# Regrouping the q products around a burst of k^T v in a linear-attention block

## The chip, the cores and the metric

The kernel runs on one core of a Trainium2 chip. The core has several engines, each with its own list of instructions that it works through in order: TensorE (PE in the profile, with PEld for its weight loads) for matrix products into PSUM, VectorE (DVE), ScalarE (ACT) and GpSimd (POOL) for the elementwise work, and SyncE (SP), whose queue here issues the transfers. Engines wait for each other through semaphores. The metric is the device time of one execution in microseconds (us), without a profile; a profiled execution is a run of its own.

## The reference

The inputs are a sequence x of 2048 tokens with 640 features, and weights, all bf16. With 32 heads of 20 features each:

```
q, k, v = split(layernorm(x) @ wqkv)                 # 640 features each
phi(a)  = concat(softmax(a @ w_phi), softmax(-(a @ w_phi)))   # per head, 40 features
o       = phi(q) @ (phi(k)^T v) / (phi(q) @ sum(phi(k)) + 1e-6)
h       = x + o @ wo
out     = h + (gelu(layernorm(h) @ w_gate) * (layernorm(h) @ w_up)) @ w_down    # 1536 wide
```

The sum over all tokens in phi(k)^T v means that no token's o can be computed before every token's k and v have been.

## The kernel before, in words

The 2048 tokens lie in 16 tiles of 128 (t), four of which make a token block of 512 (b = 0 to 3). The 640 features lie in five chunks of 128 (c).

The first stage goes over the 16 tiles. It normalises them, writes them transposed (features on partitions) into `LN1T`, multiplies v and k, takes both exps of k on ACT into `E`, and divides by the sums in `k_norm` (the multiplication at L355 is on POOL, and for some tiles half of it on DVE). The product phi(k)^T v is accumulated over all tiles in one PSUM tile, `kvp`: `kv_tile(t)` (L374) makes 32 small products for one token tile. They are not made at once for each tile but in bursts: tiles 0 to 3 at t = 9, tiles 4 to 8 at t = 13 (`KVG`), tiles 9 to 12 at t = 15 (`KVQ`, the third burst), and tiles 13 to 15 after the loop.

q needs no sum over tokens. Its product with w_phi folded in is made as 20 units: unit 5b + c is chunk c of token block b, and takes five products of 128x512 (L396), one for each chunk of the contraction. `QG` lists the units in groups. A group of one or two units shares a PSUM tile; `q_mm(j)` multiplies group j (`part` picks units of it, `kcs` contraction chunks), and `q_exp(j)` takes exp and exp of the negative on ACT (L401) into the group's tile `Eq[j]`. `QT` says that groups 0 to 3 are made at t = 15 inside the loop. `KVQ = {1: (9, 10, 11, 12)}` puts the third burst right behind group 1.

After the loop a copy on POOL (L536) reads a column of `Eq[2]`'s negative exp and writes to the gate weights' tile, so that the first loads of `Wg` (L538, on SP's queue) are held back until then. Then come the burst of tiles 13 to 15 and `kv_mask` (L381, L383, on DVE), which turns `kvp` into the block form `KV` that the second stage multiplies with.

The second stage starts with the attention of single token tiles: `attn_a(t)` multiplies phi(q) of tile t with `KV` (L585, chunks 0 to 4 with the positive exp, then chunks 0 to 4 with the negative) and copies the sums to SBUF, `attn_b` to `attn_b3` divide on DVE and form o (L686), which is transposed into `oT`, `attn_c` multiplies by `Wo` (L707), and the rest prepares the second layernorm. The remaining groups of q fill PE between the first two tiles. Then follows the gated feed-forward part (`gate_up` L767, `down` L789), which holds most of the time, with the other tiles' attention woven in.

The order on PE and on SP's queue is the order of the calls in the source; nothing reorders it. PSUM tiles of two banks come from a pool of four (`gtile`), of which `kvp` holds one until `kv_mask` has read it. A new tile waits until the engine that reads the old one is through.

The edited place, before: at t = 15 in the loop groups 0 (units 5, 6), 1 (0, 1), the third burst, 2 (2, 3), 3 (4); after the loop the last burst, and group 4 (7, 8) with `attn_a(0, 1)` between its ninth and its tenth product. `Wo` is loaded at L534 from SP's queue at t = 13.

Of the kernel before, what the change touches and what calls it, by code (L numbers as in the profile page):

```python
# [11 lines left out]
ACTF = mybir.ActivationFunctionType  # L12
# [5 lines left out]
def kernel(  # L18
# [12 lines left out]
    nc = tc.nc  # L31
# [17 lines left out]
    LQ = (7, 8, 9, 9, 10)  # L49
    FQ = (10, 11, 12, 13, 14)  # L50

    QG = ((5, 6), (0, 1), (2, 3), (4,), (7, 8), (9, 10), (11, 12), (13, 14), (15,), (16,), (17,), (18,), (19,))
    QT = (15, 15, 15, 15)
    T3 = 3

# [39 lines left out]

    Eq = [const.tile([P, len(g), 2, 512], BF16, name=f"Eq{j}") for j, g in enumerate(QG)]
    ident = const.tile([P, P], BF16, name="ident")
# [5 lines left out]
    def eq(t, c, s):  # L103
        for E, g in zip(Eq, QG):
            if t // 4 * NC + c in g:
                return E[:, g.index(t // 4 * NC + c), s, t % 4 * P:(t % 4 + 1) * P]
# [4 lines left out]
    def gtile(name):  # L111
        return psG.tile([P, 2, 512], F32, name=name, tag="G")
# [272 lines left out]
    pqs = {}  # L385

    def q_mm(j, part=(0, 1), kcs=range(NC)):

        if 0 in part and 0 in kcs:
            pqs[j] = gtile("pq")  # L390
        for i, bc in enumerate(QG[j]):
            if i not in part:
                continue
            b, c = divmod(bc, NC)
            for kc in kcs:
                nc.tensor.matmul(pqs[j][:, i, :], lhsT=Wq2[:, kc, c * P:(c + 1) * P], rhs=LN1T[b][:, kc, :],  # L396
                                 start=(kc == 0), stop=(kc == NC - 1))

    def q_exp(j, signs=(0, 1)):
        for s in signs:  # L400
            nc.scalar.activation(Eq[j][:, :, s, :], pqs[j][:, 0:len(QG[j])], ACTF.Exp, scale=(1.0, -1.0)[s])  # L401

    def st_act(t, i):

# [89 lines left out]
    for t in range(NT):  # L494
# [13 lines left out]
        for j in range(len(QT)):  # L508
            if t == QT[j]:
                q_mm(j)  # L510
                q_exp(j)
                for i in KVQ.get(j, ()):
                    kv_tile(i)
# [21 lines left out]
    q = len(QT)  # L535
# [112 lines left out]
    def attn_a(t, dve=0):  # L648
        attn_a_mm(t)
        AB, ab = ABs[t % 2], st[t, "ab"]  # L650
        for u in ((1, 0) if t in (4,) else (0, 1)):
            (nc.vector.tensor_copy if u >= 2 - dve else nc.scalar.copy)(
                AB[:, :, u * UH:(u + 1) * UH].rearrange("p s (r h) f -> p r s (h f)", r=2),
                ab[u][:, :, 0:2 * QH * KC].rearrange("p r (s x) -> p r s x", s=2))
        st[t] = AB
# [173 lines left out]


    q_mm(q, (0,))
    q_mm(q, (1,), (0, 1, 2, 3))
    attn_a(0, 1)
    q_mm(q, (1,), (4,))
    q_exp(q)
    q_mm(q + 1)
    attn_b(0, True)
    attn_b2(0, True)
    attn_b3(0)
    load_up()  # L840
    attn_a(1, 0)
    q_exp(q + 1, (0,))
    q_mm(q + 2)
    q_exp(q + 1, (1,))
# [92 lines left out]
```

## Time and profile before

| | us |
|---|---|
| median of 3 runs (lowest, highest) | 271.64 (271.57, 271.98) |
| the profiled execution | 272.4 |
| its span, first to last instruction | 270.7 |
| PE busy | 265.7 (98%) |
| DVE, ACT, POOL busy | 174.9, 138.9, 101.2 |

In a row of the chain of waits stand the start, the length, and what the end of the program was waiting for then, with a count of merged instructions. In a row of a timeline stand start, length, engine, line, operation, the tiles written and read, their sizes, the count, and in brackets the idle time before it and what ended it. A row of waits has the total, the number and the longest. A row of a group by line has the count, the busy time, the mean of one in ns, and the idle time before. A row of a stretch has, for PE, PEld, DVE, ACT and POOL, the busy time and the number of instructions, then the granted clock, the DMA share and GB/s. A row of a DMA queue has packets, MB and the share of the 16 DMA engines' time.

### The profile page before, as it was taken

To read this page: it belongs to the slowest core of one execution; us is meant where nothing else is said; L and a number is where in the kernel's file an instruction comes from. 1 tells how busy PE (TensorE), PEld (TensorE's weight loads), DVE (VectorE), ACT (ScalarE), POOL (GpSimd) and SP (SyncE) were. 2 spreads that over 40 slices of the span, in tenths; PEclk is the share of its full clock that TensorE was granted. 3 is DMA by queue.
4 is the path that set the end of the run, shared out by engine and by line. 5 is a ranking of instruction groups with operands and counts; after the bars stand their busy time and mean duration, and the time that the engine had idled before them with its cause. 6 is when DMAs were issued, how large, how long until landed. Compare 5 with 4: busy or idle time off the path is not lost.

```text
span 270.7 us, 7046 instructions
## 1 busy us (share of the span) xinstructions
PE 265.7 (98%) x2867; PEld 171.3 (63%) x2867; DVE 174.9 (65%) x347; ACT 138.9 (51%) x249; POOL 101.2 (37%) x238
## 2 busy tenths in 40 slices
PE   7999999999999999999999999999999999999995
PEld 6777777755455877788755455775555476444574
DVE  5889999996877767876466783568673332333322
ACT  5789998876789675245541356421544300322100
POOL 5548988796002335376211564014661100000000
PEclk9999999999999999999999999999999999999999
DMA  6998257250678432442201222102222101000011
GB/s 187 225 199 169 54 99 110 38 150 2 234 246 244 155 101 56 41 104 51 52 24 51 48 50 51 48 3 75 77 44 52 24 24 51 24 0 0 4 48 48
DMA packets 45264, 22.10 MB, mean 82 GB/s; under 512 B 37808, under 2 KB 43184, under 8 KB 45232
## 3 DMA queue, kind: packets, MB, share of 16 engines
q1 hardware_dynamic: 44576, 21.64, 32.6%
q8 instruction: 22, 0.36, 0.6%
q10 hardware_dynamic: 656, 0.03, 0.2%
q14 instruction: 10, 0.08, 0.1%
HBM read 10.18 MB, written 2.62 MB: 47 GB/s over the span
## 4 chain that ended last, share of the span: by engine, by line
PE 96%; DMA 2%; SPq 0%; issue 0%; DVE 0%
PE gu L767 39%; PE pd L789 19%; PE pq L396 8%; PE pk L296 8%; PE po L707 8%; PE pv L296 7%; PE kvp L374 2%; PE pv L312 2%; DMA Wv<-in_A_wqkv_dram 2%; PE ab L618 1%; PE wa L248 1%; PE ab L585 1%; PE tp L164 0%; SPq L193 0%; SPq L190 0%
## 5 line engine op out<-in xcount | busy, mean ns | idle before, releaser
L770 ACT ACTIVATE g<-gu 128x512 bf16<-128x512 f32 (+1 forms) x60 | 30.4, 510 | 73.8 <-PE gu L767 72.9
L773 DVE TENSOR_TENSOR GT<-gu,g 128x512 bf16<-128x512 f32 (+1 forms) x60 | 34.4, 580 | 46.7 <-PE gu L767 38.8
L767 PE MATMUL gu<-LN2T,Wg 128*128 128x512 bf16 (+1 forms) x300 | 61.8, 337 | 0.0
L767 PE MATMUL gu<-LN2T,Wu 128*128 128x512 bf16 (+1 forms) x300 | 61.7, 336 | 0.0
L789 PE MATMUL pd<-Wd,GT 128*128 128x320 bf16 (+4 forms) x396 | 53.9, 295 | 0.0
L789 PEld LDWEIGHTS <-GT 128*128 128x128 bf16 x396 | 37.6, 98 | 14.5 <-DVE GT L773 0.2
L767 PEld LDWEIGHTS <-Wu 128*128 128x128 bf16 x300 | 29.4, 98 | 22.6
L767 PEld LDWEIGHTS <-Wg 128*128 128x128 bf16 x300 | 29.0, 98 | 21.2
L296 PEld LDWEIGHTS <-LN1T 128*128 128x128 bf16 x290 | 27.9, 98 | 10.5
L355 POOL TENSOR_TENSOR E<-E,rs 128x640 bf16<-128x640 bf16 x25 | 31.6, 1299 | 4.4 <-DVE rs L351 4.1
L791 DVE TENSOR_TENSOR y<-pd,x_sb 128x320 bf16<-128x320 f32 (+4 forms) x33 | 15.8, 480 | 24.2 <-PE pd L789 24.2
L707 PE MATMUL po<-Wo,oT 128*128 128x320 bf16 x160 | 24.5, 299 | 0.0
L296 PE MATMUL pk<-Wk,LN1T 128*128 128x320 bf16 x160 | 24.4, 299 | 0.0
L396 PE MATMUL pq<-LN1T,Wq 128*128 128x512 bf16 x100 | 22.9, 379 | 0.0
L347 DVE TENSOR_REDUCE sk<-E 128x64 f32<-128x1280 bf16 x16 | 22.9, 1430 | 0.0
L401 ACT ACTIVATE Eq<-pq 128x1024 bf16<-128x1024 f32 (+1 forms) x26 | 19.9, 831 | 3.5 <-PE pq L396 3.3
L340 ACT ACTIVATE E<-pk 128x640 bf16<-128x640 f32 x28 | 18.7, 746 | 3.0 <-PE pk L296 3.0
L707 PEld LDWEIGHTS <-oT 128*128 128x128 bf16 x160 | 15.6, 98 | 7.3 <-ACT oT L165 0.2
L296 PE MATMUL pv<-Wv,LN1T 128*128 128x320 bf16 x130 | 19.8, 299 | 0.0
L151 ACT ACTIVATE ln<-x_sb,v,rstd 128x640 bf16<-128x640 bf16 x14 | 12.9, 920 | 13.4 <-POOL v L746 13.2
L396 PEld LDWEIGHTS <-Wq 128*128 128x128 bf16 x100 | 9.4, 98 | 10.3
L682 DVE TENSOR_TENSOR tt<-AB,w 128x1280 bf16<-128x1280 f32 x10 | 15.1, 1506 | 0.4 <-POOL w L675 0.3
(120 smaller groups left out, 290.6 us busy)
## 6 DMA issues: line engine op xcount, KB each, us to landing
out_dram<-y SPq DMA_DIRECT2D x15, 160.0 KB, 1.8
x_sb<-in_A_x_dram SPq DMA_DIRECT2D x6, 320.0 KB, 4.0
Wu<-in_B_w_up_dram SPq DMA_DIRECT2D x1, 1920.0 KB, 8.9
Wg<-in_B_w_gate_dram SPq DMA_DIRECT2D x2, 768.0 KB, 5.8
Wd<-in_B_w_down_dram SPq DMA_DIRECT2D x1, 1440.0 KB
Wo<-in_A_wo_dram SPq DMA_DIRECT2D x1, 800.0 KB, 5.2
x_sb<-in_A_x_dram SPq DMA_DIRECT2D x4, 160.0 KB, 3.3
Wv<-in_A_wqkv_dram SPq DMA_DIRECT2D x2, 320.0 KB, 4.2
```

The lines of the kernel that those rows point to most:

```text
L296: nc.tensor.matmul(ps[:, u, 0:HD], lhsT=lnT(t, c), rhs=W[:, c, u * HD:(u + 1) * HD], start=(c == 0), stop=(c == NC - 1))
L340: nc.scalar.activation(Ek[t][:, s, :].rearrange("p (u f) -> p u f", u=2), pk[:, :, 0:HD], ACTF.Exp, scale=((lnp[t][2], nrstd[t]) if t in C ...
L347: nc.vector.reduce_sum(sk, Ek[t].rearrange("p s (h f) -> p (s h) f", f=Dh), axis=AX.X)
L355: eng.tensor_tensor(e, e, rs[:, s * H:(s + 1) * H, None].to_broadcast([P, H, Dh]), ALU.mult)
L396: nc.tensor.matmul(pqs[j][:, i, :], lhsT=Wq2[:, kc, c * P:(c + 1) * P], rhs=LN1T[b][:, kc, :], start=(kc == 0), stop=(kc == NC - 1))
L401: nc.scalar.activation(Eq[j][:, :, s, :], pqs[j][:, 0:len(QG[j])], ACTF.Exp, scale=(1.0, -1.0)[s])
L707: nc.tensor.matmul(pos[u], lhsT=st[t][:, c, :], rhs=Wo[:, c, u * HD:(u + 1) * HD], start=(c == 0), stop=(c == NC - 1))
L767: nc.tensor.matmul(gu[i][:, 0:n], lhsT=W[:, c, f * P:(f + 1) * P], rhs=LN2T[b][:, c, a0:a1], start=(c == 0), stop=(c == NC - 1))
L770: nc.scalar.activation(g[:, 0:n], gu[0][:, 0:n], ACTF.Gelu_apprx_tanh)
L773: nc.vector.tensor_tensor(st[b, "g", f][:, a0:a1], gu[1][:, 0:n], g[:, 0:n], ALU.mult)
L789: nc.tensor.matmul(pd[:, 0:f1 - f0], lhsT=st[b, "g", f][:, tl * P:(tl + 1) * P], rhs=Wd[:, f, f0:f1], start=(f == 0), stop=(f == NF - 1), ...
L791: nc.vector.tensor_tensor(y[:, f0:f1], pd[:, 0:f1 - f0], x_sb[b][:, tl, f0:f1], ALU.add)
```

## The change

Group 1 becomes the single unit 7 (chunk 2 of token block 1), units 0 and 1 become group 2, units 2 and 3 group 3, and units 4 and 8 share group 4. Groups 5 to 12 stay. `KVQ`, `QT` and `T3` are as they were, so the third burst still stands behind group 1, which has five products instead of ten. `q_exp` gets an argument `part`, which takes the exps of one unit of a group. After the last burst, unit 4 is multiplied, its two exps are issued, all five products of unit 8 follow, then `attn_a(0, 1)`, then the two exps of unit 8.

On PE the order at the place is therefore: units 5, 6, 7; third burst; units 0, 1, 2, 3; last burst; units 4, 8; attention of tile 0. Before it was units 5, 6, 0, 1; third burst; 2, 3, 4; last burst; 7 and four fifths of 8; attention of tile 0; the last fifth of 8. The number of matrix products is the same. On ACT, two exps of 128x1024 become four of 128x512. The copy at L536 still reads `Eq[2]`, which is now the group of units 0 and 1.

```
-    QG = ((5, 6), (0, 1), (2, 3), (4,), (7, 8), (9, 10), (11, 12), (13, 14), (15,), (16,), (17,), (18,), (19,))
+    QG = ((5, 6), (7,), (0, 1), (2, 3), (4, 8), (9, 10), (11, 12), (13, 14), (15,), (16,), (17,), (18,), (19,))
...
-    def q_exp(j, signs=(0, 1)):
+    def q_exp(j, signs=(0, 1), part=None):
+        i = slice(0, len(QG[j])) if part is None else slice(part, part + 1)
         for s in signs:
-            nc.scalar.activation(Eq[j][:, :, s, :], pqs[j][:, 0:len(QG[j])], ACTF.Exp, scale=(1.0, -1.0)[s])
+            nc.scalar.activation(Eq[j][:, i, s, :], pqs[j][:, i], ACTF.Exp, scale=(1.0, -1.0)[s])
...
     q_mm(q, (0,))
-    q_mm(q, (1,), (0, 1, 2, 3))
+    q_exp(q, part=0)
+    q_mm(q, (1,))
     attn_a(0, 1)
-    q_mm(q, (1,), (4,))
-    q_exp(q)
+    q_exp(q, part=1)
     q_mm(q + 1)
```

## The prediction

> **What bounds the kernel now.** I read the first and third parts of the page, then what TensorE (PE) waited for, then the chain of work that ended last around the edited lines, and last the queues in that stretch.
>
> ```profile
> span 270.7 us, 7046 instructions
> PE 265.7 (98%) x2867; PEld 171.3 (63%) x2867; DVE 174.9 (65%) x347; ACT 138.9 (51%) x249; POOL 101.2 (37%) x238
> q8 instruction: 22, 0.36, 0.6%
> PE 96%; DMA 2%; SPq 0%; issue 0%; DVE 0%
> Wo<-in_A_wo_dram SPq DMA_DIRECT2D x1, 800.0 KB, 5.2
> ```
>
> PE is busy 98% of the span and is 96% of the chain. The edit adds and removes no matmul, so it can move the time only through idle time of PE. What PE waited for, in the whole execution:
>
> ```profile
> PE wu L228 <- PEq L921: 0.8, 1, 0.8
> PE kvp L374 <- issue: 0.5, 1, 0.5
> PE tp L164 <- DVE xc L272: 0.4, 1, 0.4
> PE pv L312 <- DMA Wv<-in_A_wqkv_dram: 0.4, 1, 0.4
> ```
>
> Three of the four belong to lines of the first loads and tiles. The second, 0.5 us in front of a k^T v product (L374), lies inside the third burst, the one that the change moves. The chain there:
>
> ```profile
> 57.20 4.32 PE pq L396 x20
> 61.52 0.97 PE kvp L374 x109
> 62.50 0.48 issue
> 62.98 0.30 PE kvp L374 x19
> 63.28 3.34 PE pq L396 x15
> 66.62 0.87 PE kvp L374 x96
> 67.49 2.05 PE pq L396 x9
> 69.54 0.40 PE ab L585 x38
> 69.94 1.19 PE pq L396 x5
> ```
>
> The burst has 4 token tiles of 32 products; it breaks off after 109, that is after product 13 of the fourth tile, for 0.48 us. A missing input would hold the first product of a tile, not the fourteenth, and the view puts the gap to "issue": nothing that the profile shows was waited for. So I looked at what feeds PE with instructions. Below are, for the stretches 57.2 to 60.6, 60.6 to 61.7 and 64.0 to 65.1 us, the queues that moved anything; then the number of instructions up to 62.6 us and the packets up to 62.5 us.
>
> ```profile
> q1 hardware_dynamic: 639, 0.81, 81.5%
> ...
> q8 instruction: 1, 0.02, 5.9%
> q1 hardware_dynamic: 17, 0.01, 3.7%
> ...
> q8 instruction: 1, 0.02, 5.3%
> ```
>
> ```profile
> 0.00:62.60 62.60, 60.87 (x861) 44.35 (x861) 56.94 (x107) 52.35 (x84) 47.05 (x94) 1.00 0.61 133
> ```
>
> ```profile
> q8 instruction: 6, 0.10, 0.6%
> ```
>
> PE's 2867 weight loads and 2867 products make 5734 instructions, over 22 instruction packets: about 261 each. The gap comes after 1722 of them and six packets. In the 3.4 us before 60.6 us, 0.81 MB of load traffic (the 800 KB Wo) filled 81.5% of the DMA time and no instruction packet moved; one came as soon as Wo was through, PE went on 1.3 us after that window, and the next packet came only after PE had gone on. My reading: the gap is a wait for a block of PE's own instructions, held up behind Wo. Crossing into a block is not what costs. The crossing two blocks earlier, near instruction 1722 - 2 x 261 = 1200, lay inside the burst of 160 products below, which had 1100 instructions ahead of it, and that burst ran without a break.
>
> ```profile
> 52.41 1.63 PE L374 MATMUL kvp<-E,vS 128*32 128x40 bf16 x160
> ```
>
> ```profile
> 0.00:52.45 52.45, 50.83 (x548) 37.77 (x552) 47.21 (x96) 43.85 (x72) 38.53 (x87) 1.00 0.65 137
> ```
>
> ```profile
> 56.17 0.57 SPq L534 DMA_DIRECT2D Wo<-in_A_wo_dram  x1
> ```
>
> Wo's load waits for nothing on PE, and the edit leaves all that stands before the second q group where it was. So the block comes at the same moment, 62.98 us, in both kernels.
>
> **The change, part by part.**
>
> *Five q products less ahead of the burst.* A q product takes 4.32 / 20 = 0.216 us. The burst begins at 57.20 + 15 x 0.216 = 60.44 instead of 61.52. The break keeps its place in PE's list of instructions, so the burst gets 109 + 5 = 114 products far, at 0.97 / 109 = 0.0089 us each: to 61.45. Then PE stands until 62.98: 1.53 us in place of 0.48. After it come 14 products of the burst in place of 19 (0.04 us less) and 20 q products in place of 15 (5 x 0.216 = 1.08 us more) before the last burst. That burst, and all behind it, is late by 1.08 - 0.04 = 1.04 us. From below the price is 0 (the gap moves along at 0.48 us), from above 1.08; I take 1.04, since the two ends of the wait have rows and the Wo row ties the later one to a clock that PE doesn't set.
>
> *Could the earlier burst lack its data?* The last eight normalising products on POOL are two each for tiles 11 to 13, one each for 14 and 15:
>
> ```profile
> 54.45 10.45 POOL L355 TENSOR_TENSOR E<-E,rs 128x640 bf16<-128x640 bf16 x8 [1.63 <-DVE rs L351]
> 62.19 3.39 DVE L355 TENSOR_TENSOR E<-E,rs 128x640 bf16<-128x640 bf16 x2
> ```
>
> Tile 12's second is through at 54.45 + 4 x 1.31 = 59.7, and its products come at 60.44 + 96 x 0.0089 = 61.3: 0. Tiles 14 and 15 on DVE end at 65.58, before the last burst at 62.98 + 14 x 0.0089 + 20 x 0.22 = 67.6 (20 products at 3.34 / 15 = 0.223): 0.
>
> *Chunk 4 multiplied behind the last burst, its exps between the units of its group.* In the order of instructions on PE, with the semaphores, the changed kernel has a wait that the one before lacks: the first product of chunk 8 waits for ACT, and the count that it asks for is reached by chunk 4's second exp. The two units lie in different halves of one PSUM tile, and the wait is set for the tile, whose readers must be through before it is written.
>
> ```
> 1993 L396 Ldweights Wq_102
> 1994 L396 Matmult pq<-LN1T,Wq_102 128x512 [waits Activation_49]
> ```
>
> What it costs is told by the nearest case, the last group of q in this execution, two short exps that an idle ACT starts as soon as the products are through:
>
> ```profile
> 85.37 0.59 PE L396 MATMUL pq<-LN1T,Wq 128*128 128x512 bf16 x2
> 86.00 1.09 ACT L401 ACTIVATE Eq<-pq 128x512 bf16<-128x512 f32 x2 [0.32 <-PE pq L396]
> ```
>
> PE could start the next product at 85.37 + 2 x 0.216 = 85.80; ACT starts 0.20 later and needs 1.09. So PE stands 1.29 us. From below 0 (if the wait were met early), from above 1.29 and what ACT is late. Is ACT free? With the late block, q groups (0, 1) and (2, 3) are through at 65.4 and 67.6, the last burst ends at 67.6 + 0.87 = 68.5, chunk 4 at 68.5 + 5 x 0.22 = 69.6.
>
> ```profile
> 61.56 1.94 ACT L401 ACTIVATE Eq<-pq 128x1024 bf16<-128x1024 f32 x2 [0.22 <-PE pq L396]
> L401 ACT ACTIVATE Eq<-pq 128x1024 bf16<-128x1024 f32 x14 | 13.5, 1032 | 3.0 <-PE pq L396 3.0
> L401 ACT ACTIVATE Eq<-pq 128x512 bf16<-128x512 f32 x12 | 6.5, 597 | 0.5 <-PE pq L396 0.3
> ```
>
> The two wide exps of (2, 3) run from about 67.7 to 69.7, chunk 4's could start at 69.8: just free. I take 1.29, not 0, because nothing stands on PE between the two units to hide it. Behind the waiting product stand on PE the other four of chunk 8, attn_a of tile 0, and all the rest; DVE's division and SP's transposes and last loads of Wg and Wu hang on attn_a and shift along.
>
> *The exps of chunk 4 for attn_a itself*: done before chunk 8 is even begun, so 0. *Two wide exps become four short ones*: 4 x 597 - 2 x 1032 ns = 0.32 us more on ACT, two of them inside the 1.29. The other two follow the copy of attn_a's sums, as the whole group did; ACT stood 3.0 us before wide exps for want of q products and PE now comes later still: 0, or 0.32 if ACT were full.
>
> *Ten products (and the stop) between burst and attn_a, not nine.* They cover this chain from k^T v to its masked, transposed form:
>
> ```profile
> 67.58 0.45 DVE L381 TENSOR_SCALAR KT<-kvp,sc,bi 128x160 bf16<-128x160 f32 x1 [2.00 <-PE kvp L374]
> 69.00 0.58 DVE L383 STREAM_TRANSPOSE KV<-KT 128x384 bf16<-128x384 bf16 x1
> ```
>
> It ends 69.58 - 67.49 = 2.09 us after the burst; nine products took 2.05 and attn_a's second half, which needs the end of it, comes 0.2 later, and no wait is shown. The 0.22 us more gain 0. Behind attn_a they leave one product less to cover the division of tile 0:
>
> ```profile
> 74.48 1.21 SPq L167 DMA_TRANSPOSE oT<-o  x1
> 77.52 0.84 PE L707 MATMUL po<-Wo,oT 128*128 128x320 bf16 x5
> ...
> oT<-o SPq DMA_TRANSPOSE x15, 2.4
> ```
>
> Of 3.0 us between issue and use a transpose to oT takes 2.4 in the median, and 0.2 goes: 0.4 left, cost 0, and as much as the division is later if not.
>
> *The load of Wg* is released by a copy that reads group number 2's second exp, (2, 3) before and (0, 1) now. In both it is the first group of ten products after the gap, through near 67.5, so SP's queue starts Wg when it did: 0. No transfer is added or moved past another.
>
> **Sum.** 1.04 for the block + 1.29 for the stop = 2.33 us, all on the chain, and behind them PE has no idle time that could give it back. The profiled execution took 272.4 us (span 270.7), the median of the runs is 271.64, 0.8 below; I add the shift to the median: 271.64 + 2.33 = 273.97, so 274.0 us (profiled 274.7, span 273.0).
>
> **A rule against the first term.** If blocks always lay ready, the 0.48 us would be no wait for instructions, and the sum would be 1.29 alone (rival 1). The Trainium skill, page "Runtime: NRT & Kernel Launch", section "Instruction fetch mechanics", speaks for that: instructions come in 16 KiB blocks of 256, the next is fetched while the present one runs, so that crossing a boundary is mostly hidden, and PE's store is put at 2048 instructions, eight blocks. The size of the blocks agrees with this trace's packets; the hiding does not agree with its 0.48 us behind Wo, unless that gap has another cause.
>
> **Rivals.**
> 1. *The gap is no appointment.* It is a pause of about 0.5 us tied to the instructions at that place, or no block is late and something else stops PE there; moving the burst then only trades places between it and q products on a busy PE, and 1.29 stays: 272.9 us. For it: there is one such gap to read, the view names no releaser, and the runs without a profile are 0.8 us shorter than the profiled one, more than the whole gap. Against: the uncut burst of 160, the packet right behind Wo, and that the gap is in front of no tile's first product. The page's rule above would end here. If the pause vanished as well, 271.64 + 1.29 - 0.48 = 272.5.
> 2. *ACT is late with chunk 4's exps.* It decides when the wide exps of (2, 3) end after 69.8, by what they are late; with both wide exps still to do when chunk 4 is through, 1.94 more, but they have 2.0 us since their products, so some tenths: 274.4.
> 3. *Not slower: PE doesn't set the start of the feed-forward part, a transfer does.* If the last half of the gate and up weights or the first transposed tile were what the first gate_up waits for, all that PE loses before would be made up there, as long as the loss (2.3 us) is below what the transfer is late: 271.6. For it: these loads are issued only behind oT's transpose at 74.48, and shift with it. Against: the whole list of PE's waits above has no transfer but Wv's.
>
> **Numbers.** Late block and stop 0.66, around 274.0 with its own range 273.6 to 274.3. Rival 1 0.22, at 272.5 to 273.0. Rival 2 0.07, 274.3 to 274.8. Rival 3 0.05, 271.5 to 271.8. The range 272.6 to 274.5 leaves out rival 3 and the ends of the others. About 0.2% (0.54 us) is what a measurement can tell from no change: slower 0.66 + 0.22 + 0.07 = 0.95, within 0.2% 0.04, faster 0.01 (both from rival 3).
>
> **What would show it.** Right: in the changed profile the burst starts near 60.4; PE has two new or larger idle times, about 1.5 us in front of L374, after some 114 products and ending close to 63.0, and about 1.1 us (a product's shown end is past its pace) in front of chunk 8's product at L396 with ACT's exp as the releaser; the instruction packet stands again right behind Wo; the last burst starts near 67.6 and attn_a of tile 0 near 72.0. Wrong: a gap of 0.5 us ending near 62.0, or none; no idle PE between chunk 4 and chunk 8; a Wo load at another time than 56.2; PE waiting for a transfer at the first gate_up.

## The result and the profile after

| | before | after |
|---|---|---|
| median of 6 runs each, measured beside each other (us) | 271.87 | 273.93 |
| lowest, highest | 271.57, 272.51 | 273.54, 274.31 |
| profiled execution, its span | 272.4, 270.7 | 273.88, 272.2 |

The ratio is 1.0073 with a 95% interval from 1.006 to 1.0086: 2.06 us slower, where 2.33 was forecast (274.0, range 272.6 to 274.5). The two spans differ by only 1.5 us; why is one of the questions below. Behind the edit the changed kernel's line numbers are one higher: its L402 is L401 of before, its L586 is L585.

What PE waited for in the changed kernel, in the whole execution (total, times, longest):

```profile
PE pq L396 <- ACT Eq L402: 1.2, 1, 1.2
PE wu L228 <- PEq L922: 0.8, 1, 0.8
PE kvp L374 <- issue: 0.2, 1, 0.2
```

The first row is new: a q product waits for the exp. The third is the break in the burst, shorter than before instead of longer. The timeline of PE at the place (start, length, what, count, idle time before it and its cause):

```profile
57.25 3.40 PE L396 MATMUL pq<-LN1T,Wq 128*128 128x512 bf16 x15
60.58 1.08 PE L374 MATMUL kvp<-E,vS 128*32 128x40 bf16 x114
61.92 0.27 PE L374 MATMUL kvp<-E,vS 128*32 128x40 bf16 x14 [0.25 <-issue]
62.12 4.49 PE L396 MATMUL pq<-LN1T,Wq 128*128 128x512 bf16 x20
66.54 0.94 PE L374 MATMUL kvp<-E,vS 128*32 128x40 bf16 x96
67.41 1.25 PE L396 MATMUL pq<-LN1T,Wq 128*128 128x512 bf16 x5
69.83 1.24 PE L396 MATMUL pq<-LN1T,Wq 128*128 128x512 bf16 x5 [1.17 <-ACT Eq L402]
71.01 0.47 PE L586 MATMUL ab<-KV,Eq 32*128 32x44 bf16 x40
```

The burst starts five products earlier and breaks after 114 products, as forecast, but the break ends at 61.92, not at 62.98, and the last burst starts at 66.54 and attn_a at 71.01, each about 1 us earlier than forecast. Between the fifth product of chunk 4 and the first of chunk 8 PE stands; from one start to the next there are 1.55 us where 0.216 is the pace, so the stop costs 1.34 us. On ACT, the two wide exps of group (2, 3) and the two short ones of chunk 4 run one after another, and the stop ends with the last of them:

```profile
66.65 3.14 ACT L402 ACTIVATE Eq<-pq 128x1024 bf16<-128x1024 f32 x4 [0.22 <-PE pq L396]
71.59 0.75 ACT L653 COPY AB<-ab 128x704 f32<-128x704 f32 x1 [1.81 <-issue]
```

66.65 + 3.14 = 69.79, and chunk 8 starts at 69.83. The queues from 57.2 to 60.6 us, in the changed kernel:

```profile
q1 hardware_dynamic: 592, 0.75, 76.1%
q8 instruction: 1, 0.02, 1.8%
```

The instruction packet now came in the midst of Wo's traffic, not behind it.

### The profile page after: what moved, and what is told of

Same layout as the page of the kernel before. It is cut to its first block, busy times and chain, and to the rows that moved or that the text cites. A ratio compares the mean times of both kernels' runs of the same rounds, so it can differ in the third digit from the quotient of the medians.

```text
span 272.2 us, 7047 instructions
## 1 busy us (share of the span) xinstructions
PE 266.8 (98%) x2867; PEld 172.1 (63%) x2867; DVE 174.9 (64%) x347; ACT 138.9 (51%) x251; POOL 101.0 (37%) x238
## 4 chain that ended last, share of the span: by engine, by line
PE 73%; DVE 0%; issue 0%
PE gu L768 38%; PE pd L790 19%; PE po L708 8%; PE pq L396 5%; PE ab L619 1%; PE ab L586 1%; PE tp L164 0%; PE pd L619 0%; DVE y L792 0%
## 5 line engine op out<-in xcount | busy, mean ns | idle before, releaser
L402 ACT ACTIVATE Eq<-pq 128x512 bf16<-128x512 f32 (+1 forms) x28 | 20.1, 784 | 3.5 <-PE pq L396 3.2
```

The lines of the kernel that those rows point to most:

```text
L402: nc.scalar.activation(Eq[j][:, i, s, :], pqs[j][:, i], ACTF.Exp, scale=(1.0, -1.0)[s])
```

## The experiments

The first four ran beside each other against before at 272.0 us, the last four against before at 272.42 us.

**Each half of the change alone.** The burst alone, inside group 1 of the kernel before:

```
-                q_mm(j)
-                q_exp(j)
+                q_mm(j, (0,))
                 for i in KVQ.get(j, ()):
                     kv_tile(i)
+                q_mm(j, (1,))
+                q_exp(j)
```

> The kernel before with one thing changed: the third burst stands five q products earlier, inside group 1 (unit 0, burst, unit 1, then the group's exps). No exp is split, no group changed. Theory (the break in the burst ends when a block of instructions arrives, held up by Wo's load): the break starts about 1.0 us earlier and ends where the packet lets it, 2.3 us after the packet's start, so it is longer by up to 1.0 us; time +0.4 to +1.0 us over before. Rival (the break is a pause that goes with the place in the list, or nothing on the chain): +0.0 us, break 0.5 us ending near 62.0.

Measured: 272.25 us, ratio 1.001 (0.999 to 1.0029). The twelve runs fall into two sets: six from 271.69 to 271.90, six from 272.60 to 273.66. The profiled one belongs to the second:

```profile
60.61 1.08 PE L374 MATMUL kvp<-E,vS 128*32 128x40 bf16 x114
62.34 0.27 PE L374 MATMUL kvp<-E,vS 128*32 128x40 bf16 x14 [0.65 <-issue]
```

So half of the executions are as short as most of before's, and the other half lie 0.6 to 1.7 us over the median of before; of the 29 runs of before 4 are that long (272.6 us or more). The cost is 0.25 us in the median and 0.4 in the mean (272.50 against 272.12), and the interval (-0.3 to +0.8 us) holds both the rival's 0.0 and a part of the theory's range, so the time does not decide between them. The profile does show that the break can grow: 0.83 us between starts, against 0.67 in before.

The stop alone, with groups and burst of before (`q_exp` has its new argument `part`):

```
     q_mm(q, (0,))
-    q_mm(q, (1,), (0, 1, 2, 3))
+    q_exp(q, part=0)
+    q_mm(q, (1,))
     attn_a(0, 1)
-    q_mm(q, (1,), (4,))
-    q_exp(q)
+    q_exp(q, part=1)
```

> The kernel before with the other part alone: groups and burst as before, but in group 4 (chunks 7 and 8) the exps of the first unit are issued between the two units and those of the second behind attn_a. Theory: the second unit's first product waits for the first unit's two exps, PE idle about 1.2 us there, time +1.3 us. Rival (the stop is the whole of the measured change, the block nothing): +2.1 us. Rival (the stop is made up later, since attn_a had to wait anyway): +0.0 to +0.3 us.

Measured: 274.06 us, ratio 1.0072 (1.0056 to 1.0088), +2.1 us: as much as the whole change. Its own profile says where it is more than the 1.3:

```profile
PE pq L396 <- ACT Eq L402: 1.2, 1, 1.2
PE wu L228 <- PEq L922: 0.8, 1, 0.8
PE pv L312 <- DMA Wv<-in_A_wqkv_dram: 0.7, 1, 0.7
PE po L708 <- DMA oT<-o: 0.4, 1, 0.4
PE tp L164 <- DVE xc L272: 0.2, 1, 0.2
PE kvp L374 <- issue: 0.2, 1, 0.2
```

The stop is the same 1.17 us idle (1.34 on the chain), and PE waits later for the transposed output of tile 0, whose issue on SP's queue took 2.20 us instead of 1.21:

```profile
75.88 2.20 SPq L167 DMA_TRANSPOSE oT<-o  x1
```

Against "before, Wo early" below, a kernel with no break, the parts are 0.14 us of later start, 0.34 of break, 1.34 of stop, 0.4 at the transposed output and 0.14 at the first gate_up: 2.36 of the 2.43 by which the spans differ. So the stop itself is 1.34 us, and the rival that read the whole 2.1 us as the stop is wrong by this profile. Why the issue was longer isn't settled, nor how many of the six runs had it. But the fastest of the six lies 1.94 us above the fastest of before, so the excess over 1.3 is not one stray run; that the split causes it is not shown.

**The stop taken out of the changed kernel**, with a PSUM tile of its own for the second unit:

```
     q_exp(q, part=0)
+    pqs[q] = gtile("pq")
     q_mm(q, (1,))
```

> The changed kernel, but the second unit of group 4 gets a PSUM tile of its own, so its products no longer wait for the first unit's exps. Theory: the idle time in front of chunk 8 goes, and the time falls by about 1.3 us against the changed kernel, to 272.6 us, of which 0.7 us over before is the block's; attn_a may wait up to 0.2 us for chunk 4's exps. Rival (the stop is the whole change): back to 271.9 us. Rival (the stop moves on to attn_a, which needs the same exps): stays at 273.5 us or more.

Measured: 272.45 us, ratio 1.003 (1.0007 to 1.0054), 0.15 from the forecast; ten of the twelve runs lie between 272.03 and 273.35, two at 274.46 and 275.87, which no profile explains. The wait for ACT is gone and has not moved to attn_a. The 0.45 us that are left over before are not the block's in the profiled execution, whose burst has no break. A wait took the last place that none of the three forecasts had:

```profile
PE wu L228 <- PEq L923: 0.8, 1, 0.8
PE pv L312 <- DMA Wv<-in_A_wqkv_dram: 0.4, 1, 0.4
PE gu L768 <- DMA LN2T<-ln: 0.3, 1, 0.3
```

The first gate_up waits for the transposed tile 0. Such a wait stands, shorter, in the changed kernel too: gate_up there starts 0.32 us after the start of the last attention product in front of it, against 0.12 in the kernel before, so it loses 0.20.

**The suspected cause of the break moved away: Wo at t = 10.** In the kernel before, then in the changed one, beside a second measurement of the changed kernel:

```
         if t == 10:
+            nc.sync.dma_start(Wo, wo_v)
             transpose_to(LN1T[0][:, :, P:2 * P], ln_a(1), False)
...
-        if t == 13:
-            nc.sync.dma_start(Wo, wo_v)
```

> The kernel before, with Wo's load issued three tiles earlier (t = 10 instead of 13, near 47 us), so that it is through before the instruction packet of the third burst is asked for. Theory: that packet moves near 58 to 59 us, the break in the burst is gone, time -0.3 to -0.5 us. Rival (a pause tied to the place): break of 0.5 us stays, time +0.0.

> The changed kernel once more, unaltered, as the base for the runs beside it. Theory: stop of 1.55 us between the products of chunk 4 and chunk 8 again, since it hangs on ACT alone; the break in the third burst differs from execution to execution (0 to 1.5 us), ending 2.3 us after its instruction packet starts; time +2.0 us over before. Rival (the break is tied to the place): 0.44 us again.

> The changed kernel with Wo's load issued at t = 10 instead of 13. Theory: the instruction packet of the third burst starts before 59.2 us and the burst runs without a break; the stop for ACT stays at 1.55 us; time -0.2 to -0.5 us against the changed kernel, so +1.6 to +1.8 over before. Rival (the block is nothing in the middle of the runs): +2.0 us over before, as the changed kernel.

Before with Wo early: 271.99 us, ratio 1.0 (0.9989 to 1.0012). The break is gone from the profile (span 270.07 against 270.65):

```profile
61.49 1.20 PE L374 MATMUL kvp<-E,vS 128*32 128x40 bf16 x128
```

The median doesn't fall, though -0.3 to -0.5 us was forecast. That would fit if most executions of the kernel before have little break to take away; how many have one isn't shown, since only one was profiled.

The changed kernel again: 273.76 us, ratio 1.0059 (1.0035 to 1.0082), runs from 272.92 to 275.35. That is 1.34 us over before, where +2.0 was forecast and 2.06 measured the first time. Its profiled execution is one of the long ones and shows a break of 1.03 us between starts, against 0.44 in the first profile:

```profile
58.06 3.40 PE L396 MATMUL pq<-LN1T,Wq 128*128 128x512 bf16 x15
61.39 1.08 PE L374 MATMUL kvp<-E,vS 128*32 128x40 bf16 x114
63.32 0.27 PE L374 MATMUL kvp<-E,vS 128*32 128x40 bf16 x14 [0.84 <-issue]
```

The changed kernel with Wo early: 273.51 us, ratio 1.0038 (1.0022 to 1.0054), runs from 273.03 to 274.10; that is 1.1 us over before, where 1.6 to 1.8 was forecast. The burst runs whole, the stop stays, and the four runs over 275 of the unaltered kernel have no counterpart:

```profile
60.30 1.20 PE L374 MATMUL kvp<-E,vS 128*32 128x40 bf16 x128
61.43 4.49 PE L396 MATMUL pq<-LN1T,Wq 128*128 128x512 bf16 x20
65.85 0.94 PE L374 MATMUL kvp<-E,vS 128*32 128x40 bf16 x96
66.72 1.25 PE L396 MATMUL pq<-LN1T,Wq 128*128 128x512 bf16 x5
69.14 1.24 PE L396 MATMUL pq<-LN1T,Wq 128*128 128x512 bf16 x5 [1.17 <-ACT Eq L402]
```

Moving Wo takes 0.25 us off the median and 0.5 off the mean (274.12 to 273.58); the intervals of the two ratios overlap, so this says less than the profiles do. Nor need the long runs be all break: of the 1.41 us between the two spans of the changed kernel (272.16 and 273.57), 0.81 lie ahead of the first q product, where the edit changes nothing, and 0.59 in the break.

**The wait at the first gate_up: attn_a behind nine products again, in the changed kernel.**

```
     q_exp(q, part=0)
-    q_mm(q, (1,))
+    q_mm(q, (1,), (0, 1, 2, 3))
     attn_a(0, 1)
+    q_mm(q, (1,), (4,))
     q_exp(q, part=1)
```

> The changed kernel with attn_a of tile 0 put back behind nine products instead of ten (the last product of chunk 8 follows it); exps of chunk 4 between the units as in the change, so the stop stays. Theory: what follows attn_a on DVE comes 0.2 us earlier beside PE, the transposed tile lands before the first gate_up wants it, and the 0.2 us wait of the changed kernel at the first gate_up goes: time -0.2 to -0.4 us against the changed kernel. Rival (that wait is noise of one execution): the same time as the changed kernel.

Measured: 273.72 us, ratio 1.0064 (1.0042 to 1.0086), against 273.76 for the changed kernel: no difference in time that the spread of the runs would show. In the profile gate_up starts 0.12 us after the start of the attention product in front of it, and PE waits for nothing else than the stop and the start:

```profile
PE pq L396 <- ACT Eq L402: 1.2, 1, 1.2
PE wu L228 <- PEq L923: 0.8, 1, 0.8
```

**More load traffic in the way of the packet**, in the kernel before: the first two loads of Wg directly behind Wo's, the copy on POOL left out.

> The kernel before, with the first two loads of Wg (768 KB each) issued right behind Wo's instead of behind the copy on POOL, so that more load traffic stands in the way of the instruction packet. Theory: the packet of the third burst starts later by some us, PE's break in the burst grows by 1 to 3 us and still ends 2.3 us after the packet's start; time +1 to +3 us. Rival (the break has nothing to do with load traffic): break 0 to 0.7 us as before, time +0.0, or less since Wg comes early.

Measured: 272.45 us, ratio 1.0007 (0.9983 to 1.0031). A miss for the theory as it was put: the packet started at 60.35, no later than otherwise, and the third burst ran whole. The last burst, where the next block begins, took 1.17 us instead of 0.94:

```profile
61.93 1.20 PE L374 MATMUL kvp<-E,vS 128*32 128x40 bf16 x128
63.06 3.41 PE L396 MATMUL pq<-LN1T,Wq 128*128 128x512 bf16 x15
66.41 1.17 PE L374 MATMUL kvp<-E,vS 128*32 128x40 bf16 x96
```

There PE stopped at product 94 of 96 for 0.23 us, and that block's packet had started at 64.92, 2.46 us before PE went on. In this one profile the loads queued behind Wo's did not hold up the packet beside Wo; the next, with Wg in flight, came 2.1 us after PE had entered the block ahead of it, against 1.0 to 1.6 us in the other nine profiles.

**All profiles together.** The start of the packet, read from the trace's DMA packets, and the products of the burst's last tile (in us; the fourth column is the start of the last product ahead of the break, the fifth the start of the one behind it):

| kernel | first q product | packet starts | burst reaches the block's end | PE goes on | packet to going on |
|---|---|---|---|---|---|
| before | 57.04 | 60.64 | 62.31 | 62.98 | 2.34 |
| after | 57.25 | 59.63 | 61.48 | 61.92 | 2.29 |
| after, second profile | 58.06 | 60.97 | 62.29 | 63.32 | 2.35 |
| burst alone | 57.28 | 60.04 | 61.51 | 62.34 | 2.30 |
| stop alone | 57.22 | 60.48 | 62.49 | 62.83 | 2.36 |
| two PSUM tiles | 57.20 | 58.16 | no break | | |
| nine products | 57.22 | 58.30 | no break | | |
| Wg behind Wo | 57.52 | 60.35 | no break | | |
| before, Wo early | 57.08 | 58.70 | no break | | |
| after, Wo early | 56.96 | 58.04 | no break | | |

Wherever there is a break it ends 2.3 us after the packet's start, in five profiles within 0.07 us; where the packet came early enough there is none. That is what the prediction read from one gap. What it had wrong is the packet's start: with Wo in its place it lies 1.0 to 3.6 us behind the first q product in the eight profiles, with Wo early 1.1 and 1.6 (two profiles). Two of the eight are as early as those, so that Wo's traffic makes the packet late is likely and not shown.

Why the earlier burst is more exposed can be worked out from the table. PE needs 62.31 - 57.04 = 5.27 us from the first q product to the block's end in the kernel before, and 61.48 - 57.25 = 4.23 in the changed one. Less the 2.3 us from the packet to PE's going on, a packet may lag 2.9 us behind the first q product in the one and 1.9 in the other before PE stands (an estimate). Of the eight lags with Wo in its place two exceed the first and six the second.

## Why the prediction was right, and where it was not

*The bound.* PE without idle time behind the edited place, so that each stop there is paid in full: held. The kernels without a break, with and without the stop, show it: "nine products" has a span of 271.56 us and "before, Wo early" 270.07; the first starts its q products 0.14 us later, and what is left, 1.35, is the stop's 1.34.

*The stop* (1.29 us, for chunk 4's exps in front of chunk 8): held, at 1.34. ACT began 0.2 us after the next product could have started and needed 1.09, as in the row it was taken from; the two wide exps before it were just through, as worked out.

*The late block* (1.04 us): that PE waits there for a block of its instructions held; the moment of its arrival, and with it the size, didn't. The step that failed is "So the block comes at the same moment, 62.98 us, in both kernels". It took one execution's arrival for an appointment, and that execution was a late one: 272.4 us, where half of the 29 runs of before in the first set were at or below 272.0. Over the profiles the block comes between 60.3 and 63.3 (2.3 us after the packet, also where PE did not have to wait for it). An earlier burst is exposed to more of these arrivals; that measured 0.25 us in the median and 0.4 in the mean, with an interval that holds 0. The break went from 0.67 to 0.44 us between starts in the two profiles that the prediction is compared with, so their spans differ by 1.5 us (0.21 of later start, 0.23 less break, 1.34 of stop, 0.20 at gate_up) where 2.33 was forecast. Of the prediction's own signs of being wrong two came about in the profile: a gap of about 0.5 us ending near 62.0, and PE waiting for a transfer at the first gate_up.

*One product less behind attn_a, cost 0*: wrong by 0.2 us in the profile of after. The prediction counted the transposed output (0.4 us left, and there was no wait there) and not the transfers behind it: the transposed tile for the first gate_up (`LN2T`) took from 84.25 to 87.67, with Wu's load in flight, and gate_up wanted it at 87.6. Wu's load in the kernel before, then Wu's and the transpose in the changed one:

```profile
76.36 0.42 SPq L554 DMA_DIRECT2D Wu<-in_B_w_up_dram  x1
```

```profile
77.89 0.42 SPq L555 DMA_DIRECT2D Wu<-in_B_w_up_dram  x1
84.25 1.21 SPq L167 DMA_TRANSPOSE LN2T<-ln  x1
```

The step that failed is that the transfers "shift along". The transpose itself was issued 3.4 us before gate_up could have started in both kernels. But Wu's load, which is issued behind tile 0's transposed output, came 9.7 us before that moment instead of 9.9, and took 9.1 us instead of 8.9; it landed at 87.01, and the transposed tile 0.66 us later. In all ten profiles that tile lands 0.62 to 0.67 us after Wu's load. The five with nine products ahead of attn_a lose nothing at gate_up, the five with ten lose 0.04 to 0.38 us. In the time, this 0.2 could not be shown.

*The sum.* In the first profile of after, against "before, Wo early" as a kernel with no break: 0.17 us of later start + 0.44 break + 1.34 stop + 0.20 at gate_up = 2.15, and the spans differ by 2.09 (272.16 - 270.07). For the second profile 0.98 + 1.03 + 1.34 + 0.21 = 3.56, against 3.50. In the medians, 1.34 for the stop and about 0.25 for the burst leave 0.5 us of the 2.06 of the first measurement unexplained, and they are 0.25 more than the 1.34 of the second; the two measurements of the same pair of kernels differ by that much. So it is luck that 274.0 came out so near 273.93: the block's term was about 0.8 us too high, the one at gate_up was left out, and the spread of the runs covers the rest. In the profiles, where the parts can be added up, the span of after is 272.2 and not the forecast 273.0.

*The rivals.* The pause tied to the place is refuted: no break with Wo early, breaks of 0 to 1.03 us at the same place in the list. With it falls the reading that no block is ever late: the five breaks of 0.34 to 1.03 us each end 2.3 us behind a packet. The Trainium skill's rule (page "Runtime: NRT & Kernel Launch", section "Instruction fetch mechanics") that crossing a block's boundary is mostly hidden agrees with half of these profiles and not with those five breaks. The number of that rival, 1.29 for the stop alone, is nonetheless nearer to the second measurement (1.34) than the forecast is. ACT late with the exps: did not happen. A transfer that sets the start of the feed-forward part: it did set it in the profile of after, by 0.2 us on top, and gave nothing back.

## What to carry to other kernels

In this program two units of work in one PSUM tile are one thing to the semaphores: reading the first half before the second is written makes the writer wait for the reader. Here a group that was multiplied whole before its exps had no such wait, and a split of the exps without a split of the tile cost 1.3 us on an engine without slack; look for added waits in the built order of instructions, not in the source. A gap without a releaser in the middle of very short products can be a late block of instructions: look for its packet among the loads, and take a second profile before the moment is treated as fixed.

## What was not expected of the hardware

The packet with the same place in PE's list started between 1.0 and 3.6 us after the first q product in the eight profiles with Wo's load in its place; two profiles of the unaltered changed kernel gave 2.4 and 2.9. With two more loads of 768 KB queued behind Wo it came at 2.8. What decides when it gets its turn is open. From the packet's start to PE's next product passed 2.3 us in each of the five profiles with a break, though the packet itself took about 1 us.

Tile 0's transpose into `LN2T` landed 0.62 to 0.67 us after Wu's 1920 KB, which were issued some 6 us ahead of it, in all ten profiles, whether the transpose took 2.9 or 3.6 us from issue to landing. Whether it waits for that load or shares the DMA engines with it isn't shown.
